# Joining softmax pair sums on VectorE in the last 512 queries, and halving fewer head groups of the last unit

## The chip, the cores and the metric

The kernel runs on one core of a Trainium2 chip. The metric is device microseconds of one execution; runs of a kernel are compared by their median. The engines named below are TensorE (PE, matmuls; PEld is its weight load), ScalarE (ACT), VectorE (DVE), GpSimd (POOL) and SyncE (SP, which issues the DMAs).

## The reference

A transformer block on 2048 rows of width 1024, bf16 in and out:

```
q, k, v = split(layernorm(x) @ wqkv)          # 32 heads of width 32
p = softmax(q @ k.T * 32**-0.5)               # every query against all 2048 keys
h = x + concat_heads(p @ v) @ wo
h2 = h + gelu(layernorm(h) @ w1 + b1) @ w2 + b2   # F = 3584
```

The softmax has no maximum subtracted here: the kernel computes the exponentials, the product with v and the sum of the exponentials (the denominator), and divides at the end.

## The kernel before, in words

The 2048 queries are cut into 8 units of 256 (`qb` 0 to 7); the 32 heads into 8 groups of four (`g` 0 to 7). A `Job` is the attention of one group for one unit. It has 8 rounds; a round takes 256 keys: 8 QK matmuls (four heads side by side in row strips of TensorE, L838), two exponentials of 128 x 1024 on ScalarE into one of nine PT slots (L850), and 8 PV matmuls (four heads side by side in column strips, L879) that accumulate in a PSUM bank.

The denominator accumulates in the other half of that bank, by matmuls against a vector of ones (`den`, L917). To halve them, VectorE adds the two key tiles of a round first, into one of three PS buffers (the pair sum, L894); `den` then issues four matmuls of 256 columns for that round. The job's last round skips the pair sum and issues eight matmuls straight from PT ("direct"). The sums of round r are consumed behind the PV of round r+1. `finish` divides: five small VectorE operations (L935 to L948) into OT.

A half job does 128 of the 256 queries in 4 rounds of 512 keys. Its matmuls have 128 columns, twice as many for the same work. Half jobs let the first 128 rows of a unit finish ahead of the second: before the change, groups 6 and 7 of unit 6 and groups 4 to 7 of unit 7 are done so, first all halves 0, then all halves 1.

The rest is background work on TensorE, in the order of lines 1267 to 1300: output projection of unit u (`wo`, adds x into hch), LayerNorm (`ln2`, on VectorE and POOL, then transposed into hnT), `ffn1` (28 column blocks, evicted with the bias by VectorE, L1048, then gelu: five VectorE operations and a tanh on ScalarE, L1063 to L1068), and `ffn2` in two column halves of two tiles each, evicted by L1120 and stored. The last unit's rows go through `ffn1_half(0)` and `ffn1_half(1)`, 128 rows each; the second's gelu is on ScalarE alone, after the exponentials.

The order on each engine is not written out: every operation is a task with the buffers it reads and writes, and a planner (`schedule`, `pick_pe`) plays the engines forward with estimated costs and fixes one order for each, before anything runs. On TensorE a ready QK goes first; then PV and denominators, whenever a round is ready; then background work in the order of the program. Two of the eight PSUM banks (6 and 7) are shared by jobs and background tiles; a job takes one only when 7 rounds are ready (`PV_START`), so that its PV comes in a burst, and a background tile does not take the last free one while 6 are ready. On VectorE, pair sums have priority -2, `finish` -1 and 0, evictions 0, gelu 1.

`FOURS` is an empty tuple before the change, so the branches that test it are dead.

## Time and profile before

| | us |
|---|---|
| median of 3 runs | 1082.41 (1079.09 to 1084.54) |
| the profiled execution, whole | 1077.0 |
| its span | 1075.2 |
| TensorE / ScalarE / VectorE busy | 1048.8 / 1007.8 / 762.0 |
| last exponential ends | 1015.2 |

Times in the trace run from the start of the span. "Idle before" is the time for which an engine stood before a group of instructions, with the one that released it. The mean duration of an instruction includes its latency, so instructions in a row take less than their number times the mean. The granted TensorE clock is 1.00 throughout. Attention of unit 6 begins near 757 us, of unit 7 near 884; the half jobs of unit 6 run from about 852 to 884, those of unit 7 from about 948 to 1015.

### The profile page before, as it was taken

How to read it: one execution, taken by the hardware profiler on the slowest of the kernel's cores; microseconds unless marked ns; L12 is line 12 of the kernel's file. 1: busy time of each engine (PE TensorE's matmuls, PEld its weight loads, DVE VectorE, ACT ScalarE, POOL GpSimd, SP SyncE). 2: the span in 40 equal slices, each digit the busy share in tenths (PEclk: the TensorE clock that was granted, in tenths of full speed). 3: DMA queues.
4: the chain of work that ended last, by engine and by line, in shares of the span. 5: the costliest groups of instructions: out<-in, count | busy, mean ns of one | idle time of the engine just before them, and what ended most of it. 6: DMA issues, size and time to landing. Idle time of an engine off the chain costs nothing.

```text
span 1075.2 us, 40898 instructions
## 1 busy us (share of the span) xinstructions
PE 1048.8 (98%) x18598; PEld 612.0 (57%) x18598; DVE 762.0 (71%) x1493; ACT 1007.8 (94%) x1117; POOL 47.1 (4%) x110
## 2 busy tenths in 40 slices
PE   8999999999999999999999999999999999999998
PEld 6576555554445744654574466457446644664675
DVE  8766666566677995797599579759957956885660
ACT  4999999999999999999999999999999999999731
POOL 4200000000000010001001000100000001000000
PEclk9999999999999999999999999999999999999999
DMA  8461544334665546746664774655477444864640
GB/s 218 128 182 25 178 132 119 120 119 159 212 206 161 188 154 214 256 170 204 196 211 158 214 258 168 210 193 196 134 212 274 157 166 163 276 242 169 229 162 16
DMA packets 130654, 192.12 MB, mean 179 GB/s; under 512 B 47024, under 2 KB 95024, under 8 KB 127920
## 3 DMA queue, kind: packets, MB, share of 16 engines
q1 hardware_dynamic: 130480, 189.50, 54.2%
q8 instruction: 146, 2.39, 0.9%
q14 instruction: 28, 0.23, 0.1%
HBM read 175.32 MB, written 26.21 MB: 187 GB/s over the span
## 4 chain that ended last, share of the span: by engine, by line
ACT 57%; PE 36%; DMA 3%; DVE 2%; issue 1%; POOL 0%; SPq 0%; DVEq 0%
ACT PT L850 53%; PE ps L599 16%; PE ps L838 5%; PE ps L596 5%; PE ps L879 4%; PE ps L602 3%; ACT uu L1066 2%; PE ps L917 2%; ACT PX L850 2%; DMA a_w2r<-w_blocks 2%; DMA a_w1r<-w_blocks 1%; DVE PS L894 1%; DMA xrb<-in_A_x_dram 1%; DVE st L648 0%; DVE hch L1120 0%
## 5 line engine op out<-in xcount | busy, mean ns | idle before, releaser
L850 ACT ACTIVATE PT<-ps 128x1024 bf16<-128x1024 f32 x992 | 924.1, 1184 | 11.6 <-PE ps L838 9.4
L894 DVE TENSOR_TENSOR PS<-PT 128x1024 bf16<-128x1024 bf16 x425 | 276.6, 684 | 85.2 <-PE ps L917 52.4
L838 PE MATMUL ps<-QT,KT 32*128 32x256 bf16 (+1 forms) x4480 | 204.2, 263 | 8.2 <-ACT PT L850 4.9
L879 PE MATMUL ps<-PT,V 128*32 128x256 bf16 (+1 forms) x4352 | 163.6, 264 | 2.0 <-DVE hch L1120 0.8
L838 PEld LDWEIGHTS ps<-QT,KT 32*128 32x128 bf16 x4480 | 66.5, 92 | 162.3 <-ACT PT L850 148.1
L599 PE MATMUL ps<-a_w2r,gT 128*128 128x512 bf16 x598 | 148.5, 381 | 1.6 <-DVE gT L1048 0.8
L599 PE MATMUL ps<-hnT,a_w1r 128*128 128x256 bf16 x1134 | 139.2, 273 | 0.3 <-DVE hnT L678 0.2
L599 PEld LDWEIGHTS ps<-hnT,a_w1r 128*128 128x128 bf16 x1134 | 104.4, 98 | 29.3 <-issue 16.0
L917 PE MATMUL ps<-PS,ones 128*32 128x256 bf16 (+1 forms) x1876 | 118.4, 266 | 2.1 <-issue 1.4
L879 PEld LDWEIGHTS ps<-PT,V 128*32 128x32 bf16 x4352 | 102.7, 97 | 26.1 <-issue 8.9
L599 PEld LDWEIGHTS ps<-a_w2r,gT 128*128 128x128 bf16 x598 | 51.2, 98 | 68.7 <-issue 16.2
L1048 DVE TENSOR_TENSOR gT<-ps,b1f 128x512 bf16<-128x512 f32 x98 | 67.3, 686 | 23.3 <-PE ps L596 12.8
L599 PE MATMUL ps<-xnT,Wall 128*128 128x512 bf16 (+1 forms) x364 | 79.9, 355 | 0.4 <-ACT xnT L676 0.2
L1120 DVE SCALAR_TENSOR_TENSOR hch<-ps,hch 128x512 bf16<-128x512 f32 x32 | 21.9, 683 | 77.6 <-PE ps L599 39.5
L1066 ACT ACTIVATE uu<-uu 128x1024 bf16<-128x1024 bf16 (+1 forms) x53 | 61.3, 1181 | 10.5 <-DVE uu L1065 10.5
L596 PE MATMUL ps<-hnT,a_w1r 128*32 128x256 bf16 x1736 | 64.7, 274 | 2.6 <-issue 1.7
L917 PEld LDWEIGHTS ps<-PS,ones 128*32 128x32 bf16 x1876 | 47.3, 96 | 20.7 <-issue 7.7
L599 PE MATMUL ps<-wov,OT 128*128 128x512 bf16 x222 | 55.4, 380 | 0.0
L596 PE MATMUL ps<-a_w2r,gT 128*32 128x512 bf16 x744 | 53.2, 381 | 2.1 <-issue 1.4
L596 PEld LDWEIGHTS ps<-hnT,a_w1r 128*32 128x32 bf16 x1736 | 43.9, 96 | 13.6 <-issue 11.5
L599 PEld LDWEIGHTS ps<-xnT,Wall 128*128 128x128 bf16 x364 | 31.3, 98 | 32.9 <-issue 9.5
L653 POOL CAST mvb<-mv 128x2 bf16<-128x2 f32 (+1 forms) x25 | 5.8, 231 | 985.0 <-DVE mv L650 985.0
(101 smaller groups left out, 970.9 us busy)
## 6 DMA issues: line engine op xcount, KB each, us to landing
a_w2r<-w_blocks SPq DMA_DIRECT2D x105, 512.0 KB, 4.6
a_w1r<-w_blocks SPq DMA_DIRECT2D x98, 512.0 KB, 4.2
wov<-wo_blocks SPq DMA_DIRECT2D x16, 1024.0 KB, 4.8
w_blocks<-in_B_w_dram SPq DMA_DIRECT2D x28, 512.0 KB, 3.9
w1b<-w_blocks SPq DMA_DIRECT2D x14, 512.0 KB, 3.9
Wall<-in_A_wqkv_dram SPq DMA_DIRECT2D x17, 256.0 KB, 4.3
xrb<-in_A_x_dram SPq DMA_DIRECT2D x16, 256.0 KB, 4.9
a_w1r<-in_A_wqkv_dram SPq DMA_DIRECT2D x8, 512.0 KB, 4.8
```

What stands on the lines that cost most here:

```text
L596: fns.append(lambda p, j=j: p.matmul(psum[32 * j:32 * j + 32, bi(bank), c0:c1], lhsT[:, 32 * j:32 * j + 32], rhs, start=start, stop=stop, ...
L599: t.whole = lambda p: p.matmul(psum[:, bi(bank), c0:c1], lhsT, rhs, start=start, stop=stop, skip_group_check=True)
L602: t = pe(lambda p: p.matmul(psum[:, bi(bank), c0:c1], lhsT, rhs, start=start, stop=stop), occ, reads=reads, writes=[bb(bank)], mode="full" ...
L653: pool(lambda g: g.tensor_copy(mvb[:, sl, :], mv_l[:, sl, :]), 0.25, reads=B_mv[sl], writes=B_mvb[sl], prio=prio)
L838: return p.matmul(psum[:, 2 * us[h // 2] + h % 2, n * i:n * i + n], KT[32 * h:32 * h + 32, g, k0:k0 + P], QT[32 * h:32 * h + 32, qs, q0:q0 ...
L850: act(lambda a, u=u, k=k: a.activation(PTs[s][:, k, :, :], psum[:, 2 * u:2 * u + 2, :], ACT.Exp, bias=0.0, scale=SCALE), 1024, reads=[B_ps ...
L879: fns.append(lambda p, i=i, h=h: p.matmul(psum[32 * h:32 * h + 32, bi(bank), 0:nq], V[:, g, kt * r + i, 32 * h:32 * h + 32], PTs[s][:, h / ...
L894: dve(lambda v: v.tensor_tensor(PS[:, n, :, :], pairs[:, :, 0:256], pairs[:, :, 256:512], ALU.add), c_dve(1024, 2), reads=B_PTs[s], writes ...
L917: fns.append(lambda p, h=h, rhs=rhs, i=i: p.matmul(psum[32 * h:32 * h + 32, bi(bank), 256:256 + nq], ones32[:, :], rhs, start=False, stop= ...
L1048: t = dve(lambda v: v.tensor_tensor(g[:, fc:fc + nf, :], psum[:, bi(bank), :].rearrange("p (f c) -> p f c", f=nf), b1f[:, fc:fc + nf].unsq ...
L1066: act(lambda a: a.activation(w, w, ACT.Tanh, bias=0.0, scale=KT2), m, reads=[B_uu[i]], writes=[B_uu[i]], prio=-1)
L1120: drop(dve(lambda v: v.scalar_tensor_tensor(hch[:, hs, c], psum[:, bi(bank), :], half, hch[:, hs, c], ALU.mult, ALU.add), c_dve_ps(512), r ...
```

## The change

In units 6 and 7 (`qb >= 6`, the last 512 queries), in full jobs alone: the pair sum of an even round 0, 2 or 4 is kept in its PS buffer; that of the following round is made as before, and then the kept one is added to it on VectorE, in place, at the pair sums' priority. One `den` of four matmuls then serves both rounds. Round 6 keeps its own pair sum, round 7 stays direct. So a full job has 4 + 2 groups of four denominator matmuls instead of 7 + 2, and three more VectorE additions of 128 x 1024.

In unit 7, groups 4 and 5 become full jobs; only groups 6 and 7 are done in halves, as in unit 6.

```diff
-    FOURS = ()
+    FOURS = (0, 2, 4)
...
-                if nq == 256 and r in FOURS:
+                four = nq == 256 and self.qb >= 6
+                if four and r in FOURS:
                     self.half = n
-                elif nq == 256 and r - 1 in FOURS:
+                elif four and r - 1 in FOURS:
                     o = self.half
                     dve(lambda v: v.tensor_tensor(PS[:, n, :, :], PS[:, n, :, :], PS[:, o, :, :], ALU.add), c_dve(1024, 2),
                         reads=[B_PS[n], B_PS[o]], writes=[B_PS[n]], prio=-2)
...
-        attention(u + 3, range(G) if u < 3 else range(6) if u == 3 else range(4))
+        attention(u + 3, range(G) if u < 3 else range(6) if u == 3 else range(6))
...
-    attention_half(7, range(4, G), 0)
-    attention_half(7, range(4, G), 1)
+    attention_half(7, range(6, G), 0)
+    attention_half(7, range(6, G), 1)
```

## The prediction

> **What bounds the kernel now.** I read the page first, for engines and slices.

> ```profile
> PE 1048.8 (98%) x18598; PEld 612.0 (57%) x18598; DVE 762.0 (71%) x1493; ACT 1007.8 (94%) x1117; POOL 47.1 (4%) x110
> DVE  8766666566677995797599579759957956885660
> ACT  4999999999999999999999999999999999999731
> q8 instruction: 146, 2.39, 0.9%
> L894 DVE TENSOR_TENSOR PS<-PT 128x1024 bf16<-128x1024 bf16 x425 | 276.6, 684 | 85.2 <-PE ps L917 52.4 <-ACT PT L850 29.1
> ```

> TensorE (98%) and ScalarE (94%) are both nearly full. ScalarE runs exponentials until its third slice from the end; TensorE fills the gaps with projections and the FFN and carries the last 57 us alone. VectorE looks free at 71%, but its slices swing between 5 and 9. So I asked for busy time in stretches cut at the stage borders (columns: stretch, length, then busy us of PE, PEld, DVE, ACT, POOL, each with its instructions).

> ```profile
> 757.00:822.50 65.50, 64.00 (x1018) 31.35 (x1019) 45.19 (x89) 64.74 (x72) 3.08 (x8) 1.00 0.62 190
> 822.50:865.00 42.50, 41.36 (x791) 27.65 (x789) 39.27 (x74) 42.49 (x47) 0.00 (x0) 1.00 0.50 179
> 884.00:927.50 43.50, 41.69 (x727) 21.31 (x725) 29.19 (x58) 43.50 (x48) 3.69 (x8) 1.00 0.56 193
> 927.50:965.00 37.50, 35.58 (x849) 26.05 (x841) 34.33 (x65) 35.81 (x40) 0.00 (x0) 1.00 0.73 256
> ```

> The second and the fourth hold FFN-1 with its gelu on VectorE. There VectorE has 3.2 us to spare in each; elsewhere 14 to 20.

> Third, the timeline, for what TensorE waits for where it stops (start, length, engine, work, idle time before).

> ```profile
> 877.72 0.28 PE L917 MATMUL ps<-PS,ones 128*32 128x128 bf16 x6
> 879.37 0.23 PE L917 MATMUL ps<-PS,ones 128*32 128x128 bf16 x2 [1.37 <-issue]
> ...
> 917.96 0.40 PE L838 MATMUL ps<-QT,KT 32*128 32x256 bf16 x8 [0.45 <-ACT PT L850]
> 918.37 0.62 PE L669 MATMUL ps<-ident,a_xb 128*128 128x128 bf16 x8
> 919.79 0.40 PE L838 MATMUL ps<-QT,KT 32*128 32x256 bf16 x8 [0.80 <-ACT PT L850]
> 920.39 1.36 PE L599 MATMUL ps<-hnT,a_w1r 128*128 128x256 bf16 x11 [0.20 <-DVE hnT L678]
> ...
> 970.91 0.63 PE L879 MATMUL ps<-PT,V 128*32 128x128 bf16 x32 [0.80 <-DVE hch L1120]
> ...
> 1017.97 12.68 PE L599 MATMUL ps<-hnT,w1b 128*128 128x128 bf16 x224
> ```

> At 917.5 to 920.4 TensorE has no background work: it waits for the LayerNorm of unit 6, which hangs on the end of unit 6's attention, paced by ScalarE. At 971 a PV burst waits for a PSUM bank until VectorE evicts an FFN-2 tile. At 877.7 one task of eight matmuls is cut after six, with no semaphore between. From 1018 on nothing but TensorE's own sequence is left, and it begins with the FFN-1 of the last unit's first 128 rows.

> In VectorE's timeline that FFN-1's input is complete at 1012.2:

> ```profile
> 1011.48 0.69 DVE L678 COPY hnT<-ps 128x1024 bf16<-128x1024 bf16 x1 [2.24 <-PE ps L669]
> ```

> **The change, part by part.** The sum is made against the profiled execution, 1077.0 us (span 1075.2). The runs shown have the median 1082.41, 5.4 us above it, so I carry the difference over to that. Runs of this kernel spread by 0.5% (1079.09 to 1084.54), so within 0.5%, 5.4 us, a change can't be told from none.

> *Denominator matmuls.* A full job has seven pair sums, each with four matmuls against the ones vector side by side, 0.11 us from start to start (898.57 to 898.68), and one direct group of 0.22. Joining rounds 0-1, 2-3, 4-5 removes three of the seven. Ten jobs are full before and after (unit 6 groups 0 to 5, unit 7 groups 0 to 3): 10 x 3 x 0.11 = 3.3 us. Groups 4 and 5 of unit 7 turn from two half jobs (6 x 0.11 + 2 x 0.22 = 1.10) into one full one (4 x 0.11 + 0.22 = 0.66): 0.9 us. QK and PV take the same 0.33 and 0.22 a round in both forms. TensorE sheds 4.2 us. But what is shed before 917 (six jobs of unit 6 and the first two of unit 7, 8 x 0.33 = 2.6) only lengthens the wait for unit 6's LayerNorm, which ScalarE sets. I count -1.6; the bounds are 0 and -4.2.

> *Joins on VectorE.* 12 jobs x 3 joins, 0.62 us each (four pair sums of the same size took 2.49): 22 us. Groups 4 and 5 have one more pair sum each (1.2) and one finish of five operations less (two of 1.32 against one of 1.87, so -1.5 in all). In the stretches without gelu this lies in idle time; if that cover were gone it would all delay evictions. The joins fit the three PS buffers: a join frees one, so rounds 0 to 3 and 5 can be summed ahead of the burst, and three operations (sum 4, the last join, sum 6) stand behind its start where four pair sums stood. In 822 to 865 the bursts at 832 and 848 bring 3.7 us against 3.2 spare; 0.5 late there vanishes in the wait at 917. In 927 to 965 there come seven joins (the last of group 2, three each of groups 3 and 4), 4.3 us, and four pair sums of group 4 that stood at 971 before, 2.5: 6.8 against 3.2 spare. Sums and joins have priority over evictions, and those over gelu, so the last gelu ends 3.6 us later, at about 972.5 instead of 968.9. Behind it wait FFN-2's last chunk, its eviction, and the PSUM bank for the next PV burst. Bounds: 0 (the other FFN-2 tile fills in) to 3.6 (all of it idle); -1.8 if ScalarE's 1.78 us wait at 971 also goes. I take +2.0, as TensorE already idled 2.7 us in 957 to 980 for want of such cover.

> *Fewer halves: the instruction stream.* Two half jobs issue 336 matmuls for one group, the joined full job 152, so 368 fewer, and 120 fewer in the ten other jobs, each with its weight load. Cuts inside one task, as at 877.7 (1.37 us), came at 962.9 (0.75) and 1006.8 (1.42) too, all among half jobs. Unit 7's stretch of halves shrinks from 67 us (948 to 1015) to 37: of 2.2 us, 1.2 stay. I take -1.0, between 0 and -2.2.

> [...]

> *Fewer halves: the tail.* Half 0 of the last unit is done when 32 exponentials are still to come; now 16, so 16 x 0.924 = 14.8 us later, against the 5.8 us by which hnT (1012.2) was ahead of its first use (1018.0). The way from half 0's last exponential (984.2) to hnT took 28.0 us, most of it waiting: the burst until seven rounds were ready, the output projection until 1002.7 for banks. Its work alone is a burst of 1.7, the finish 1.3, 16 matmuls of 0.213 (3.4), an eviction of 0.7, and from the LayerNorm's first statistics to hnT 6.2 (1035.27 to 1041.4) to 8.7 (1003.5 to 1012.2): 13.3 to 15.8. From 1015.2 - 14.8 = 1000.4 that gives 1013.7 to 1016.2, in time: 0. With all 28.0 it is 1028.4, 10.4 late, of which the second half's output projection (3.7), free to go first, fills some: 6.7. I take +2.0, nearer the short end, since TensorE has little else to put ahead by then.

> *Queues.* The diff adds or removes no DMA. The query loads of groups 4 and 5 go out once as before. The weights that take over the K and V of groups 4 and 5 can start some 20 us sooner, on SP, which is not full. POOL's one-element operations for the last unit's first LayerNorm move later with it, in the tail term.

> Sum: -1.6 + 2.0 - 1.0 + 2.0 = +1.4 us: 1078.4 against the profiled 1077.0, and 1083.8 against the median.

> **The rivals.** *The banks are tied up (slower).* At the end of FFN-1 of unit 6 both tiles of FFN-2 take the two PSUM banks and wait for the late gelu. Group 4's seven rounds are ready at about 948.3 + 14 x 0.924 + two tanh of 0.95 = 963.1; its PV has no bank; two rounds later (966.8) the nine PT slots are full and ScalarE stops until the tile is evicted, 972.5 + 0.85 + 0.7 = 974.0: 7.2 us in place of my 2.0, 1089.0. It decides if both tiles are begun before 963 and the gelu ends after 965. For it: 970.91 is this wait, and ScalarE lost 1.78 there. Against: the planner keeps the second bank free once six rounds are ready.

> *The tail is uncovered (slower).* All 6.7 us: 1.4 - 2.0 + 6.7 = +6.1, 1088.5, if hnT is later than the last other work of TensorE. For it: the 28 us chain; against: its 13 to 16 us of work.

> *Everything shed counts (faster).* 4.2 saved and 2.2 of cuts gone, joins and tail hidden: -6.4, 1076.0. For it: TensorE is busy 98%. Against: the wait at 917 and VectorE's 3.2 us.

> The joins can't fail to happen: they are fixed in the instruction order.

> **How the numbers follow.** Near no change 0.54 (1083.8, its own range 1077 to 1087.8); banks 0.17; tail 0.13; everything shed counts 0.16. So faster by over 0.5% 0.16, within 0.54, slower 0.30. The range runs from 1076.5, inside the fast rival, to 1091, beyond both slow ones by the 2 us in which they may add to each other; about 2 in 10 stay outside, most of it below.

> **What would show it.** Right: L917 on PS,ones with 120 fewer matmuls of 256 columns in the ten jobs; 36 new TENSOR_TENSOR of about 0.62 us from PS to PS; a longer wait near 917; the last gelu of FFN-1 of unit 6 near 972; hnT of the last unit's first rows near the end of the exponentials. Wrong: ScalarE standing for more than 3 us near 965 to 975 (banks); TensorE idle for more than 4 us between 1003 and 1020 (tail); or FFN-1 of unit 6 starting 3 us sooner (all of it counts). Another order from the planner, with other pauses, would make all four terms wrong together.

## The result and the profile after

The changed kernel takes 1076.41 us (median of 10 runs, 1072.61 to 1078.2) against 1080.7 us for the kernel before (10 runs, 1077.14 to 1085.01). The ratio is 0.9956, with a 95% interval of 0.9938 to 0.9974: 4.7 us less, between 2.8 and 6.7. That is within the 0.5% that I had called "no change", yet the interval excludes none at all. I had forecast 1.4 us more, and the time lies 0.1 us below my range. The two profiled executions, 1077.0 and 1075.0 us, show only 2.0 us of the difference, so what follows rests on runs more than on these two traces.

The page of the changed kernel, on the lines shown of before:

```profile
PE 1043.1 (97%) x17978; PEld 605.2 (56%) x17978; DVE 783.6 (73%) x1521; ACT 1008.1 (94%) x1117; POOL 49.1 (5%) x110
DVE  8766666566677995797499569759978958987560
ACT  4999999999999999999999999999999999999732
q8 instruction: 141, 2.31, 0.8%
L894 DVE TENSOR_TENSOR PS<-PT 128x1024 bf16<-128x1024 bf16 x427 | 280.2, 685 | 76.9 <-PE ps L918 39.0
```

TensorE is 5.7 us less busy, VectorE 21.6 us more (I had worked out 22). TensorE has 620 matmuls fewer on record: 488 are those that I counted, the other 132 come from the planner, which now issues 44 background matmuls whole that stood as four column strips each (L596 has 176 fewer, L599 44 more). The instruction queue, q8, brings 141 packets instead of 146.

Busy time in stretches of the changed kernel (stretch, length, then busy us of PE, PEld, DVE, ACT, POOL with their instructions; clock, DMA share, GB/s):

```profile
822.50:865.00 42.50, 41.23 (x743) 27.37 (x740) 41.56 (x80) 42.27 (x47) 0.00 (x0) 1.00 0.51 177
884.00:927.50 43.50, 39.73 (x784) 21.49 (x784) 36.83 (x75) 43.50 (x49) 3.76 (x8) 1.00 0.56 187
927.50:965.00 37.50, 35.27 (x747) 24.64 (x744) 33.50 (x62) 35.54 (x40) 0.00 (x0) 1.00 0.75 269
965.00:985.00 20.00, 16.36 (x224) 7.06 (x220) 16.43 (x32) 20.00 (x23) 0.00 (x0) 1.00 0.72 246
```

VectorE's spare time in 822 to 865 is down from 3.2 us to 0.9. TensorE stands 3.8 us in 884 to 927.5 where it stood 1.8 before: at least a part of the shed work turns into waiting there. In 965 to 985 it stands 3.6 us (1.8 before), while ScalarE, which stood 1.8 us in that stretch, does not stand at all. Before, that stretch read:

```profile
965.00:985.00 20.00, 18.20 (x527) 9.69 (x519) 10.21 (x24) 18.22 (x21) 0.00 (x0) 1.00 0.43 153
```

TensorE's timeline of the changed kernel at the places that the prediction named (start, length, work, idle time before):

```profile
877.58 0.28 PE L879 MATMUL ps<-PT,V 128*32 128x128 bf16 x6
879.01 0.34 PE L879 MATMUL ps<-PT,V 128*32 128x128 bf16 x10 [1.16 <-issue]
...
918.68 0.40 PE L838 MATMUL ps<-QT,KT 32*128 32x256 bf16 x8 [0.71 <-ACT PT L850]
919.51 1.14 PE L599 MATMUL ps<-hnT,a_w1r 128*128 128x256 bf16 x9 [0.43 <-DVE hnT L678]
...
977.64 0.59 PE L599 MATMUL ps<-a_w2r,gT 128*128 128x512 bf16 x2 [1.57 <-DVE gT L1069]
...
997.24 0.35 PE L838 MATMUL ps<-QT,KT 32*128 32x128 bf16 x12
998.01 0.23 PE L838 MATMUL ps<-QT,KT 32*128 32x128 bf16 x4 [0.43 <-issue]
...
1017.23 2.23 PE L599 MATMUL ps<-hnT,w1b 128*128 128x128 bf16 x37
1020.15 10.60 PE L599 MATMUL ps<-hnT,w1b 128*128 128x128 bf16 x187 [0.69 <-issue]
```

FFN-1 of unit 6 starts at 919.5 instead of 920.4. FFN-2 waits for a gelu before 977.6. The last unit's FFN-1 starts at 1017.2 instead of 1018.0. Three tasks are cut inside, at 878, 997 and 1019, with no wait that the profile knows ("issue").

VectorE's timeline of the changed kernel gives the inputs behind these starts:

```profile
976.81 0.69 DVE L1069 TENSOR_TENSOR gT<-uu,gT 128x1024 bf16<-128x1024 bf16 x1
...
980.20 0.69 DVE L1069 TENSOR_TENSOR gT<-uu,gT 128x1024 bf16<-128x1024 bf16 x1
...
1016.35 0.69 DVE L678 COPY hnT<-ps 128x1024 bf16<-128x1024 bf16 x1
```

The gelu that FFN-2 waited for is the last but one; it ends at 977.5. The last gelu of unit 6 ends at 980.9, 12 us later than before, where VectorE's timeline has it at:

```profile
968.26 0.69 DVE L1068 TENSOR_TENSOR gT<-uu,gT 128x1024 bf16<-128x1024 bf16 x1
```

The first half's hnT is complete at 1017.0 instead of 1012.2, still 0.2 us ahead of its use.

### The profile page after: what moved, and what is told of

The parts are those of the page before. It is cut to its first block, busy times and chain, and to the rows that moved or that the text cites. A ratio compares the mean times of both kernels' runs of the same rounds, so it can differ in the third digit from the quotient of the medians.

```text
span 1073.2 us, 39708 instructions
## 1 busy us (share of the span) xinstructions
PE 1043.1 (97%) x17978; PEld 605.2 (56%) x17978; DVE 783.6 (73%) x1521; ACT 1008.1 (94%) x1117; POOL 49.1 (5%) x110
## 4 chain that ended last, share of the span: by engine, by line
PE 61%; ACT 31%; DMA 3%; DVE 3%; issue 1%; POOL 0%; SPq 0%; DVEq 0%; POOLq 0%
PE ps L599 29%; ACT PT L850 28%; PE ps L838 10%; PE ps L596 7%; PE ps L879 7%; PE ps L918 4%; PE ps L602 3%; ACT PX L850 2%; DMA a_w2r<-w_blocks 2%; ACT uu L1067 2%; DMA a_w1r<-w_blocks 1%; DVE PS L894 1%; PE ps L1144 1%; PE ps L669 0%; DVE hch L1121 0%
## 5 line engine op out<-in xcount | busy, mean ns | idle before, releaser
L850 ACT ACTIVATE PT<-ps 128x1024 bf16<-128x1024 f32 x992 | 924.6, 1176 | 9.1 <-PE ps L838 8.6
L894 DVE TENSOR_TENSOR PS<-PT 128x1024 bf16<-128x1024 bf16 x427 | 280.2, 685 | 76.9 <-PE ps L918 39.0
L838 PE MATMUL ps<-QT,KT 32*128 32x256 bf16 (+1 forms) x4352 | 203.6, 266 | 9.3 <-ACT PT L850 6.6
L879 PE MATMUL ps<-PT,V 128*32 128x256 bf16 (+1 forms) x4224 | 160.6, 267 | 3.0 <-ACT PT L850 1.8
L838 PEld LDWEIGHTS ps<-QT,KT 32*128 32x128 bf16 x4352 | 64.4, 92 | 163.9 <-ACT PT L850 149.4
L599 PE MATMUL ps<-a_w2r,gT 128*128 128x512 bf16 x609 | 152.1, 381 | 4.5 <-DVE gT L1069 1.6
L599 PE MATMUL ps<-hnT,a_w1r 128*128 128x256 bf16 x1165 | 143.3, 273 | 2.7 <-DMA a_w1r<-w_blocks 2.2
L599 PEld LDWEIGHTS ps<-hnT,a_w1r 128*128 128x128 bf16 x1165 | 107.0, 98 | 33.6 <-issue 17.8
L879 PEld LDWEIGHTS ps<-PT,V 128*32 128x32 bf16 x4224 | 101.5, 97 | 25.7 <-issue 8.9
L918 PE MATMUL ps<-PS,ones 128*32 128x256 bf16 (+1 forms) x1692 | 108.7, 268 | 1.0 <-DVE PS L894 0.8
L599 PEld LDWEIGHTS ps<-a_w2r,gT 128*128 128x128 bf16 x609 | 52.0, 98 | 74.7 <-issue 19.7
L599 PE MATMUL ps<-xnT,Wall 128*128 128x512 bf16 (+1 forms) x364 | 79.9, 355 | 0.2 <-ACT xnT L676 0.2
L1067 ACT ACTIVATE uu<-uu 128x1024 bf16<-128x1024 bf16 (+1 forms) x53 | 61.6, 1182 | 14.2 <-DVE uu L1066 14.2
L596 PE MATMUL ps<-hnT,a_w1r 128*32 128x256 bf16 x1612 | 61.0, 274 | 2.1 <-issue 1.7
L599 PE MATMUL ps<-wov,OT 128*128 128x512 bf16 x224 | 56.0, 380 | 0.0
L918 PEld LDWEIGHTS ps<-PS,ones 128*32 128x32 bf16 x1692 | 43.0, 96 | 18.9 <-DVE PS L894 6.7
L596 PE MATMUL ps<-a_w2r,gT 128*32 128x512 bf16 x700 | 50.2, 381 | 0.0
L599 PEld LDWEIGHTS ps<-xnT,Wall 128*128 128x128 bf16 x364 | 31.2, 98 | 32.8 <-issue 9.6
L596 PEld LDWEIGHTS ps<-hnT,a_w1r 128*32 128x32 bf16 x1612 | 40.8, 96 | 12.4 <-issue 10.7
```

The costliest lines, as they stand in the source:

```text
L596: fns.append(lambda p, j=j: p.matmul(psum[32 * j:32 * j + 32, bi(bank), c0:c1], lhsT[:, 32 * j:32 * j + 32], rhs, start=start, stop=stop, ...
L599: t.whole = lambda p: p.matmul(psum[:, bi(bank), c0:c1], lhsT, rhs, start=start, stop=stop, skip_group_check=True)
L838: return p.matmul(psum[:, 2 * us[h // 2] + h % 2, n * i:n * i + n], KT[32 * h:32 * h + 32, g, k0:k0 + P], QT[32 * h:32 * h + 32, qs, q0:q0 ...
L850: act(lambda a, u=u, k=k: a.activation(PTs[s][:, k, :, :], psum[:, 2 * u:2 * u + 2, :], ACT.Exp, bias=0.0, scale=SCALE), 1024, reads=[B_ps ...
L879: fns.append(lambda p, i=i, h=h: p.matmul(psum[32 * h:32 * h + 32, bi(bank), 0:nq], V[:, g, kt * r + i, 32 * h:32 * h + 32], PTs[s][:, h / ...
L894: dve(lambda v: v.tensor_tensor(PS[:, n, :, :], pairs[:, :, 0:256], pairs[:, :, 256:512], ALU.add), c_dve(1024, 2), reads=B_PTs[s], writes ...
```

## The experiments

Ratios are to runs of the kernel before that were made alongside on the same chip, in brackets the 95% interval. "Tail" is the span after the last exponential. "Cuts" is the sum of TensorE's stops beyond 740 us that the profile puts down to "issue" and that fall on the places described below, inside a task or between two; a stop counts when over 0.5 us pass from one matmul's start to the next, less 0.1 us each for the regular step. Both come from the one profiled execution of a kernel, so they are rougher than the times.

**Each part alone.** The joins without the new order of groups (the edit is to the changed kernel):

```diff
-        attention(u + 3, range(G) if u < 3 else range(6) if u == 3 else range(6))
+        attention(u + 3, range(G) if u < 3 else range(6) if u == 3 else range(4))
...
-    attention_half(7, range(6, G), 0)
+    attention_half(7, range(4, G), 0)
```

(and the same for half 1); and the new order without the joins (to the kernel before):

```diff
-        attention(u + 3, range(G) if u < 3 else range(6) if u == 3 else range(4))
+        attention(u + 3, range(G) if u < 3 else range(6) if u == 3 else range(6))
...
-    attention_half(7, range(4, G), 0)
+    attention_half(7, range(6, G), 0)
```

> The joins alone: rounds 0 to 5 joined two by two in the ten full jobs of units 6 and 7, groups 4 to 7 of unit 7 still in halves. TensorE sheds 10 x 3 x 0.11 = 3.3 us, VectorE gets 30 x 0.62 = 18.6 us more. Theory 'ScalarE sets the end' (the time is the end of the last exponential plus a fixed 58 us, and the changed kernel gained because the exponentials lost 4.1 us less among half jobs): nothing, -1 to +1 us, since the halves stay. Rival 'TensorE's work sets the end': -2 to -3.3 us.

> Fewer halves alone: groups 4 and 5 of unit 7 full, no joins. TensorE sheds 2 x 0.11 = 0.2 us, and 512 matmuls of 128 columns become 256 of 256. Theory 'ScalarE sets the end': -3 to -4.5 us, nearly the whole effect, with the exponentials' stalls near 963, 971 and 1008 gone. Rival 'TensorE's work sets the end': -0.5 to +2 us, as the tail loses cover and next to nothing is shed.

The joins alone took 1.0027 [1.0000, 1.0054], the new order alone 1.0021 [0.9998, 1.0045]: +2.9 and +2.3 us, where both together take −4.7. No sum explains that. My first theory after the result, that the time follows the moment at which ScalarE ends and that the order of the last groups brings it forward, fell here.

**VectorE's load alone.** To the kernel before, in full jobs of units 6 and 7, the pair sum of rounds 1, 3 and 5 is made a second time, which loads VectorE as the joins do and takes nothing off TensorE:

```diff
+                if nq == 256 and self.qb >= 6 and r in (1, 3, 5):
+                    dve(lambda v: v.tensor_tensor(PS[:, n, :, :], pairs[:, :, 0:256], pairs[:, :, 256:512], ALU.add), c_dve(1024, 2),
+                        reads=B_PTs[s], writes=[B_PS[n]], prio=-2)
```

> The kernel before, with the pair sums of rounds 1, 3 and 5 made twice in the ten full jobs of units 6 and 7: the joins' load on VectorE (30 x 0.62 = 18.6 us) with nothing shed on TensorE and the halves as they were. It is the price of the joins by itself. My prediction's term: +0 to +3.6 us, +2 taken. Theory 'ScalarE sets the end': 0 to +1, as long as the exponentials do not stop longer near 970. If VectorE does not matter at all: within 1 us of before.

It took 0.9993 [0.9971, 1.0015]. Its VectorE is nearly as full as that of the change, by stretches:

```profile
822.50:865.00 42.50, 40.32 (x950) 29.84 (x942) 39.91 (x80) 42.50 (x47) 0.00 (x0) 1.00 0.62 197
884.00:927.50 43.50, 41.96 (x909) 21.17 (x910) 35.22 (x71) 43.50 (x49) 3.05 (x8) 1.00 0.56 180
...
965.00:985.00 20.00, 18.42 (x514) 10.83 (x516) 16.11 (x36) 19.58 (x23) 0.00 (x0) 1.00 0.38 136
```

and its last gelu is as late:

```profile
980.80 0.69 DVE L1071 TENSOR_TENSOR gT<-uu,gT 128x1024 bf16<-128x1024 bf16 x1
```

The gelu ends 12.5 us later than before, and the kernel takes no longer: at this place of the instruction stream neither the load on VectorE nor the lateness behind it cost anything that twelve runs could find.

**The matmuls put back.** In the changed kernel the joined sum is fed to the denominator twice, so TensorE does the work that the joins shed, 12 jobs x 12 matmuls, while VectorE's joins and the order of the groups stay. The denominator then counts rounds 0 to 5 double, so the output is not that of the block; the kernel serves for its time alone:

```diff
                 elif four and r - 1 in FOURS:
...
+                    self.sums.append((n, False))
                     self.sums.append((n, False))
```

> The changed kernel with each joined sum multiplied by ones twice (the denominator counts rounds 0 to 5 double): TensorE gets back 12 x 3 x 0.11 = 4.0 us, all else stays. Theory 'ScalarE sets the end': it stays at the changed kernel's gain, -3.5 to -5 us against before. Rival 'TensorE's work sets the end': back to before, -1 to +1 us.

It took 0.9994 [0.9972, 1.0016]: 4.1 us more than the change, give or take 3, where 144 matmuls at 0.028 us (0.11 us from start to start for four) are worth 4.0. In its trace FFN-1 of unit 6 starts at 921.8 us, 2.3 us later than in the change. So the shed matmuls seem to count in this kernel. The edit is not that alone, though: the planner now issues 74 background matmuls whole that the change has in strips, so TensorE has 78 matmuls fewer on record, not 144 more, and all that follows stands elsewhere in its instruction stream. That leaves the question why the joins alone, which shed 3.3 us of matmuls in ten jobs, were not faster.

**The place in the instruction stream.** What spoke against a sum was already visible before any edit takes effect. At about 630 us the kernels differ in nothing, and one task is cut in all six of them. Here is TensorE's timeline of the kernel before:

```profile
629.28 0.61 PE L596 MATMUL ps<-hnT,a_w1r 128*32 128x256 bf16 x16
631.42 0.51 PE L596 MATMUL ps<-hnT,a_w1r 128*32 128x256 bf16 x12 [1.52 <-issue]
```

and of the joins alone:

```profile
630.45 0.61 PE L596 MATMUL ps<-hnT,a_w1r 128*32 128x256 bf16 x16
632.43 0.51 PE L596 MATMUL ps<-hnT,a_w1r 128*32 128x256 bf16 x12 [1.37 <-issue]
```

I numbered the records of TensorE (matmuls, weight loads and some 140 of its sequencer) in order. In the six kernels so far, all 38 cuts of over 0.5 us inside a task fall on records 193 to 195 of a block of 256. The packets of q8, of 16.4 KB, fit: 146 for the 37,335 records of the kernel before, which are 145.8 blocks, and 141 for the 36,096 of the changed kernel, which are 141.0. If the cuts belong to such blocks, a kernel that does the same in the same order, with all its instructions moved by half a block, must be cut elsewhere. To move them, warm-up matmuls at the start are split, so that the same columns take more instructions: 128 places (`s128`), 64 (`k < 32`) or 192 (four parts).

```diff
-        pe(lambda p: p.matmul(psum[:, 6, 0:256], ident[:, :], b2t[:, 0:256], start=True, stop=True), 0.18 if k < 42 else 0.115,
+        parts = 2 if k < 64 else 1
+        pe([lambda p, c=c, w=256 // parts: p.matmul(psum[:, 6, c * w:c * w + w], ident[:, :], b2t[:, c * w:c * w + w], start=True, stop=True)
+            for c in range(parts)], 0.18 if k < 42 else 0.115,
```

> The kernel before, with 64 of the 80 warm-up matmuls at the start split into two of 128 columns: the same work in the same order, but every later TensorE instruction stands 128 places further on. Theory 'block cuts' (TensorE's stream stops at fixed places 256 instructions apart, in all traces so far at the same remainder, 193; where such a place falls among dense matmuls the kernel loses 0.5 to 3 us): another time than before, by 1 to 4 us, either way, with the cuts 64 matmuls away in the work from 877.8, 946.8, 962.7 and 1006.4. Rival 'TensorE's work': within 1 us of before.

> The changed kernel with the same shift by 128 places. Theory 'block cuts': it loses part of its gain, -3 to +2 us against before, as the changed kernel had drawn a good place for its cuts (4.0 us in all behind 740, before 5.2). Rival 'TensorE's work': -4 to -5.5 us as without the shift.

> The joins alone, shifted by 128 places. Unshifted it was 2.9 us slower than before, with cuts of 2.45, 1.27 and 2.92 us at 992, 1022 and 1027. Theory 'block cuts': better by 2 to 5 us, -3 to +1 us against before. Rival 'the joins' load on VectorE or the tail makes it slower': +2 to +4 us as before.

> Fewer halves alone, shifted by 128 places. Unshifted it was 2.3 us slower than before, with cuts of 2.2 and 3.3 us at 951 and 1014. Theory 'block cuts': better by 2 to 5 us, -3 to +1 us against before. Rival 'the tail loses its cover': +2 to +4 us as before.

The four kernels moved by 128 have no cut at 630. They have one at 568, where no unmoved kernel has any. TensorE's timeline of the kernel before, moved by 128:

```profile
568.09 0.28 PE L917 MATMUL ps<-PT,ones 128*32 128x256 bf16 x3
569.25 0.39 PE L917 MATMUL ps<-PT,ones 128*32 128x256 bf16 x5 [0.89 <-issue]
```

and of the changed kernel, moved by 128:

```profile
568.43 0.28 PE L918 MATMUL ps<-PT,ones 128*32 128x256 bf16 x3
569.80 0.39 PE L918 MATMUL ps<-PT,ones 128*32 128x256 bf16 x5 [1.09 <-issue]
```

The same eight matmuls are cut after the third in all four. So the cuts belong to places in the instruction stream, and the move alone made the kernel before 1.0072 [1.0045, 1.0098].

The traces also show what stands ahead of a cut. In all twenty of this document there are 142 cuts of over 0.5 us inside a task. All fall on records 193 to 196 of a block, if a weight load stands for its matmul too (the moved kernels lack some 70 matmul records). And ahead of every one a packet of q8 starts 2.2 to 3.7 us before TensorE goes on, in the median 2.35; where the kernel before crosses without a stop, it starts some 5 us ahead in the median. I read this as TensorE standing until its next block of instructions has come; what the traces show is the times, not what is in a packet.

**Four places, to average them out.** The other two places:

> The kernel before, shifted by 64 places (32 warm-up matmuls split in two). With before (0) and before_s128 (+7.5 us) it shows how far the place of the cuts alone moves this kernel. Theory 'block cuts': somewhere within -3 to +9 us of before, with cuts 32 matmuls earlier in the work than before's; no theory of the change's own says anything but 0.

> The kernel before, shifted by 192 places (32 warm-up matmuls split in four). As before_s64: -3 to +9 us by the theory of the cuts, 0 without it.

> The changed kernel shifted by 64 places. If the change has a gain of its own, apart from the place of the cuts, the mean of the changed kernel over the four shifts lies 3 to 8 us under the mean of the kernel before over the same four; if its 4.7 us were luck with the cuts, the two means are within 2 us. For this run: -6 to +3 us against before.

> The changed kernel shifted by 192 places; as after_s64: -6 to +3 us against before, and with the others the mean over four places of the cuts.

> The joins alone, shifted by 64 places. If the joins bring most of the gain (3.3 us less on TensorE, 240 fewer of its instructions): the mean over four places is 4 to 8 us under that of the kernel before (whose four are 0, +3.6, +7.8, +12.1 us), so about -3 to +2 here. If they bring about half, as 0 and 128 say (-3.0 in the mean): -1 to +4 here.

> The joins alone, shifted by 192 places: with the mean over four places as for joins_only_s64, +4 to +9 us here if the joins bring 3 to 8 us, +12 if nothing.

> Fewer halves alone, shifted by 64 places. At 0 and 128 they bring nothing in the mean (+2.3 against 0, +5.6 against +7.8). If that holds: +2 to +6 us here; if fewer halves bring the gain by taking 512 TensorE instructions out of the dense stretch: -4 to 0.

> Fewer halves alone, shifted by 192 places: +9 to +13 us if they bring nothing in the mean, +2 to +7 if they do by thinning the stream.

Ratios to the unmoved kernel before, each known to about ±0.0024, and means over the four places (±0.0012), with the mean cuts and tail of the four profiles:

| moved by | 0 | 64 | 128 | 192 | mean | in us | cuts, us | tail, us |
|---|---|---|---|---|---|---|---|---|
| before | 1 | 1.0033 | 1.0072 | 1.0112 | 1.0054 | +5.9 | 9.1 | 61.6 |
| joins alone | 1.0027 | 1.0050 | 0.9988 | 1.0039 | 1.0026 | +2.8 | 6.6 | 62.7 |
| new order alone | 1.0021 | 1.0069 | 1.0052 | 1.0124 | 1.0067 | +7.2 | 11.3 | 63.0 |
| the change | 0.9956 | 1.0003 | 0.9968 | 1.0016 | 0.9986 | −1.5 | 4.2 | 60.7 |

The kernel before happens to stand at its best place of the four. From place to place the change is worth 4.7, 3.2, 11 and 10 us, on average 7.4 ± 2 by the noise of the runs; the places themselves scatter by 4, so four of them fix the mean less well than that. The joins alone are worth 3.0, near the 3.3 that they shed; the new order alone costs 1.3. Together they give 5.7 ± 2.6 us more than their sum, and that excess itself is 10, 9, 0 and 4 us by place. A cut in a crowded stretch looks like this; TensorE's timeline of the kernel before, moved by 192:

```profile
993.90 0.39 PE L917 MATMUL ps<-PT,ones 128*32 128x128 bf16 x13
997.05 0.24 PE L917 MATMUL ps<-PT,ones 128*32 128x128 bf16 x3 [2.76 <-issue]
```

**The matmuls put back, at a second place.**

> The changed kernel with each joined sum multiplied by ones twice (the denominator counts rounds 0 to 5 double), shifted by 128 places: 144 groups less thin, 4.0 us of TensorE's work and its instructions back, joins and fewer halves as they are. Unshifted it gave back 4.1 us of the gain. If the denominator matmuls that the joins remove carry the gain (their time, and their instructions in the bursts): +0.3 to +1.0% above after_s128 (0.9968), so 1.000 to 1.007. If fewer halves or the place alone carry it: 0.995 to 0.999.

1.0024 [1.0008, 1.0041], 6.1 us more than the change at that place; with the 4.1 at the first, 5.1 ± 2 on average. Its cuts are 4.7 us at these two places against 2.3 for the change, and its tail is 2 to 4 us longer. Less the cuts, 2.7 us are left for 4.0 us of work, so how much of the work counts is known only roughly.

**Joins in units 3 to 7** (the changed kernel with `self.qb >= 3` in place of `>= 6`):

> The changed kernel with the joins in units 3 to 7 instead of 6 and 7: 24 more full jobs, so 24 x 0.33 = 7.9 us less on TensorE and 45 us more on VectorE before 757. If TensorE's work sets the time there: 3 to 8 us faster than the changed kernel. If ScalarE sets it there (its exponentials lose next to nothing before 757): within 2 us of the changed kernel, or slower by what gelu waits longer for VectorE; the cuts fall at other places, which alone can move it by 5 us.

0.9980 [0.9961, 0.9998]: not better than the change, though it sheds 24 jobs' worth more of matmuls. What TensorE sheds before unit 6 is not worth a gain that these runs, at one place of the stream, could find.

## Why the prediction was wrong, point by point

I forecast +1.4 us and −4.7 came. The steps that failed are the two prices of +2.0, for waits behind the joins on VectorE and for the later tail: the waits are in the trace or just avoided, but next to nothing of them reached the end (−0.8 and +0.2 us measured). After them comes the size of the shed matmuls (−1.6, where 4.1 came back at this place). The sum of the parts as measured at this place, −4.1, −0.8, −1.2 of cuts and +0.2, is −5.9, which agrees with −4.7 within the noise (the 4.1 holds some cuts of its own, so the parts are not quite apart).

*Denominator matmuls (−1.6): probably too small.* I had argued that what is shed before 917 only lengthens the wait for unit 6's LayerNorm. The change shows much of that (TensorE stands 3.8 us in 884 to 927.5 instead of 1.8, and FFN-1 of unit 6 starts only 0.9 us sooner). But with the matmuls put back into the change 4.1 and 6.1 us came back, against 4.0 of work, and FFN-1 of unit 6 started 2.3 and 3.4 us later. By these runs the term is more like −2.7 to −4, known to about 2; the rest that comes back fits the longer cuts and tail.

*Joins on VectorE (+2.0): this step failed; −0.8 [−3.1, +1.6] us in the run with the sums made twice.* I had the work right and the lateness of the last gelu too small (12 us, not 3.6), and still the lateness cost nothing. In the trace it is not free of waits: TensorE stands 1.6 us for the last gelu but one at 977.6, where it stood 0.8 us for a bank at 971 before. Why such waits do not reach the end is not tested; I would argue that the second half's attention and output projection, which come later anyway, stand ready to fill what the waits push back. The rival of the tied-up banks needed a gelu that ends after 965, and got it at 980.9, but ScalarE stood 0.0 us in 965 to 985: it did not run out of PT slots.

*Fewer halves, the instruction stream (−1.0): right in size by luck, wrong in cause.* I had read the cuts as a matter of half jobs, and taken them away with these; the cut at 631 us of the kernel before, far from any half job, already spoke against it. At the place at which the kernels were compared the cuts fell from 4.8 to 3.6 us. But the new order alone, which takes away the same half jobs, has 11.3 us of cuts on average over the four places, more than the kernel before (9.1); the joins alone have 6.6 and the change 4.2. So on average the cuts fell by 4.9 us, and with the joins. And they depend on where the blocks of 256 fall: near 878 there is a cut after as before, in another task, at record 29,634 instead of 29,890, exactly one block of 256 earlier. A crossing from one block of 256 records to the next mostly goes by without a stop: of 146 crossings of the kernel before only 5 bring a cut of over 0.5 us inside a task. But where one did stop TensorE, it was for up to 3.3 us (the new order alone, at 1014).

*Fewer halves, the tail (+2.0): this step failed; +0.2 in the change.* hnT came 4.9 us later, 0.2 us ahead of its use, so the short end of my bounds was right (tail 60.2 against 60.0 us in the profiles at the unmoved place). In the new order alone the mean tail is 1.4 us longer.

*Queues (0): a wait that I did not price.* In the traces TensorE waits for weights of FFN-1 between 925 and 970 us, 2.3 us on average over the four places of the change against 0.8 before. What that costs at the end was not tested.

*The sum.* Over four places −7.4 us is roughly 4 of shed matmuls and 4.9 of cuts, of which some 2 are given back elsewhere, perhaps in that wait. At the one place at which the kernels were compared it is −4.7. The rival "everything shed counts" (−6.4) was nearest, and its chance of 0.16 too low: its two terms are the ones that were found. Its own time, 1076.0, lay just outside my range, and its sign did not come: FFN-1 of unit 6 started 0.9 us sooner, not 3.

*What stays open.* Why the cuts fall with the joins. It is not the number of instructions alone: the joins alone have 18,406 matmuls and 6.6 us of cuts, the new order alone 18,209 and 11.3. The matmuls put back bring back 2.4 us of cuts. A guess, not tested: a crossing costs nothing where TensorE waits anyway, and the joins make such waits. Nor is it settled whether the 5.7 us by which both parts together exceed their sum are more than four places can average out.

## What to carry to other kernels

Where one engine issues densely, as TensorE does here (97 to 98% busy), compare two kernels at several places of their instruction stream before a per cent is ascribed to an edit: here the place alone moved the same kernel by up to 1.1%, more than the edit. Late work with low priority behind a full VectorE cost nothing that the runs could find (the last gelu 12.5 us later, ratio 0.9993), although a trace shows waits for it, so measure such a load by itself, by doing it twice. What TensorE shed in the last two units counted (with 4.0 us of it put back, 4.1 and 6.1 us came back), though how much of it is known only roughly; the same shed in units 3 to 5 brought nothing that these runs could find (0.9980, against 0.9956 without it).

## What the runs showed of the hardware

Around the longest stops the granted clock read 0.50. In the new order alone, a cut of 3.13 us follows a wait of 1.13; TensorE's timeline:

```profile
1014.12 0.28 PE L838 MATMUL ps<-QT,KT 32*128 32x128 bf16 x5 [1.13 <-ACT PT L850]
1017.53 0.50 PE L838 MATMUL ps<-QT,KT 32*128 32x128 bf16 x11 [3.13 <-issue]
```

and the clock (the third number from the right) in the stretches around it:

```profile
1010.00:1015.00 5.00, 2.50 (x128) 1.87 (x128) 3.46 (x13) 4.28 (x5) 0.00 (x0) 0.99 0.95 330
1015.00:1020.00 5.00, 2.47 (x16) 0.96 (x17) 0.69 (x1) 1.92 (x2) 0.00 (x0) 0.50 0.79 243
```

The joins alone show the same behind 943 to 946, a wait of 3.34 us for a weight transfer: 1.00 in 940 to 945, 0.50 in 945 to 950. All five stops and waits of over 3 us in these traces came with a clock of 0.50 for over 3 us, which began during them or up to 1.7 us behind. Shorter ones were at times (2.03 us before 795 in the kernel before, moved by 64) and at times not (2.52 us before 942 with the sums made twice), so these traces give no length of stop from which on it happens. Of 135 runs of the kernel before, the 55 with a mean clock of 1.000 have the median 1081.1 us, the 80 with less 1084.2; whether such stops make this difference was not tested.
